# Attention and two expert layers on one core: V of the first batch pooled by products with a matrix of ones, more filler products, two normalisations moved to ScalarE, and a new list of slots

## The chip, the cores and the metric

The kernel runs on one core of one Trainium2 chip, as one program with one launch. The metric is device time in microseconds (us), from the first instruction to the last and what lies around them; the number before is a median of three runs. The engines are TensorE (PE, with its weight loads PEld), VectorE (DVE), ScalarE (ACT), GpSimd (POOL) and SyncE (SP), whose queue issues the DMAs.

## The reference

8 batches, 8 heads, 576 tokens, head size 64. K and V are averaged over groups of 8 tokens, which leaves 72 keys and 72 values for each head. The attended tokens (4608 of 512 numbers) go through two expert layers of 512 to 2048 to 512.

```python
k_p = k.reshape(B, H, Sp, pool, D).mean(axis=3)          # pool = 8, Sp = 72
v_p = v.reshape(B, H, Sp, pool, D).mean(axis=3)
scores = scale * np.matmul(q, k_p.transpose(0, 1, 3, 2))
scores = scores - np.max(scores, axis=-1, keepdims=True)
attn = np.exp(scores)
attn = attn / (np.sum(attn, axis=-1, keepdims=True) + 1e-09)
x = np.matmul(attn, v_p)                                 # then (4608, 512)
h = x @ w_in;   x = np.maximum(0.01 * h, h) @ w_out                  # layer 1
h = x @ w2_in;  x = (h * np.clip(h + 3.0, 0.0, 6.0) / 6.0) @ w2_out  # layer 2
```

## The kernel before

**Units of attention.** There are 24 units, three for each batch: unit 3b and unit 3b+1 take four heads each and the first 384 tokens (each with keys and values of its own to load), unit 3b+2 the other 192 tokens of all eight heads. A unit runs `scores` (products with the keys; a maximum, exponentials and sums in two halves of 432 columns; the normalisation at L633), `transposes` (L659), `transpose_rem` (L681; the last 8 keys of each head are handled apart) and `values` (L710). K is pooled by a reduction on DVE (L404). V is pooled so too, but for the first two units, `early`, TensorE does it in `pool_v` (L431): eight products with the identity, added up in PSUM, one for each token of a group of eight, first for 64 of the pooled values (128 columns each, `u.vs`) and then for the last 8 (32 partitions, 64 columns, `u.rs`). The copies of `u.vs` and the product of `u.rs` with a mask (L481) follow.

**Halves of the exponentials.** A half (number 2 times its unit, plus 0 or 1) is done in one of two ways: six exponentials on ACT, each with its maximum as bias and its sum read out (L599); or, where its number is in `C["sub"]`, a subtraction on DVE (L584), one exponential on ACT (L588) and a reduction on DVE (L591).

**The layers.** Layer 1 of the first 896 tokens is done by `moe_tile` in three passes: tokens 0 to 383 with the first 8 of 16 slices of the weights, tokens 384 to 895 with all 16, tokens 0 to 383 with the other 8. Meanwhile the weights are decoded and turned into the operands of a seven-product scheme, which are stored in DRAM (`first_weights`, `pair_weights`, `second_weights`, tensors `left...`). The other tokens of layer 1 and all of layer 2 go in nine `Pair`s of token blocks with those operands (L1158), streamed back from DRAM. The units of attention are spread over the three passes and the first pairs.

**The order.** The kernel is written as tasks with an engine, a cost and dependencies. A job is attached to a slot (one step of a pass or of a pair) by the tables in `C`, which sets the order in which tasks are written down and so which buffer each gets. `Plan.order` then simulates the engines with the costs, ranks the tasks by how long they may be delayed, and writes one fixed order for each engine; `flex` says up to which task a copy may go to either ACT or DVE. Up to `fill_until` (the third step of the first pass) it puts filler products of 128 zero columns (`self.fill`, L1654) in TensorE's queue: as many as fit a planned gap, and twelve more after a run of `weak` tasks (transposes, the scores of units 3b+2, the last 8 values). A filler is an instruction like others: if the gap is shorter than planned, what is behind it waits.

```python
out += [self.fill] * int((self.starts[i] - busy - 200) / 56)
busy = self.starts[i] + cost
if i in self.weak and weak > 1500:
    out += [self.fill] * 12
    weak = 0.0
weak = weak + cost if i in self.weak else 0.0
```

Of the kernel before, what the change touches and what calls it, by code (L numbers as in the profile page):

```python
# [16 lines left out]
ALU = mybir.AluOpType  # L17
AX = mybir.AxisListType

B, H, S, D = 8, 8, 576, 64  # L20
DM, DFF = 512, 2048
POOL, SP = 8, 72
# [9 lines left out]
C = dict(  # L32
    n32=4,
    soon={0: 0, 1: 0, 2: 2000},
    flex=715,
    mid=8,
    halves=9,
    sub=[1, 2, 3, 13, 20, 23],
    parts=31,
    when0=[0, 1, 0, 2, 5, 3, 10],  # L40
    att0=[0, 4, 8],
    gaps0=[0, 0, 2, 2, 0],
    when1=[4, 10, 20, 26],
    att1=[0, 7, 14, 22],
    gaps1=[0, 3, 3, 3, 0],
    att2=[0, 5],
    gaps2=[0, 1, 5, 6, 0],
    prep2=[26, 68],
    att=[[4, 26, 42, 51], [10, 24, 39, 58, 70], [0, 21, 40, 55], []],
    gaps=[[0, 7, 7, 11, 2], [0, 11, 9, 19, 1], [0, 2, 10, 11, 6], [7, 14, 2, 4, 4]],  # L50
    prep=[[85, 106], [94, 89], [102, 89], [84, 93]],
    left1=[[(0, 65)], [(1, 0), (2, 1), (3, 16)]],
    left2=[[], [], [(0, 40)], [(1, 23), (2, 45)], [(3, 18), (4, 39)], [(5, 23), (6, 40)], [(7, 15)]],
)
SCORES = 1500
WIDE_SCORES = 1400
# [50 lines left out]
class Plan:  # L107
# [102 lines left out]
    def order(self):  # L210
        n = len(self.tasks)
        ways, after = zip(*self.tasks)
        then = [[] for _ in range(n)]
        for i in range(n):
            for j in after[i]:
                then[j].append(i)

        due, pe = [0.0] * n, 0.0
        for i in range(n - 1, -1, -1):
            engine, cost, _ = ways[i][0]  # L220
            due[i] = min((due[j] - self.lag(engine, ways[j][0][0]) - self.extra[i] for j in then[i]), default=0.0)
            if engine == "pe":
                due[i] = pe = min(due[i], pe) - cost
            else:
                due[i] -= cost
        sooner = lambda rank: [r - self.sooner.get(i, 0) for i, r in enumerate(rank)]
        rank = sooner(i if w[0][0] == "pe" else d for i, (w, d) in enumerate(zip(ways, due)))
        back = lambda a, b: self.lag(b, a)
        self.end = None
        for _ in range(ROUNDS):  # L230
            starts, way, end = self.place(ways, after, then, rank, self.lag, FIRST)
            chosen = [w[k] for w, k in zip(ways, way)]
            if self.end is None or end < self.end:
                self.end, self.starts, self.chosen = end, starts, chosen
            late = [-s - w[1] for s, w in zip(starts, chosen)]
            starts, _, _ = self.place([[w] for w in chosen], then, after, late, back, {}, True)
            rank = sooner(-s - w[1] for s, w in zip(starts, chosen))
        self.idle = []
        out, busy, weak = [], WARM_FROM, 0.0
        for i in sorted(range(n), key=lambda i: (self.starts[i], i)):  # L240
            engine, cost, emit = self.chosen[i]
            if engine == "pe" and busy is not None:
                out += [self.fill] * int((self.starts[i] - busy - 200) / 56)
                busy = self.starts[i] + cost
                if i in self.weak and weak > 1500:
                    out += [self.fill] * 12
                    weak = 0.0
                weak = weak + cost if i in self.weak else 0.0
                if i == self.fill_until:
                    busy = None  # L250
            out.append(emit)
            self.idle.append((self.starts[i], i))
        return out


@with_exitstack
def attention_moe_moe(ctx: ExitStack, tc: tile.TileContext, qt, kt, vm, vr, wt, wq, eye, mask, out):

# [39 lines left out]
    def on_pe(n, emit, reads, writes, weak=False):  # L300
        if weak:
            plan.weak.add(len(plan.tasks))
        add("pe", n, emit, reads, writes)
# [25 lines left out]
    def load(dst, src, nbytes):  # L329

        on_dma(nbytes * (FIRST_LOADS if len(plan.tasks) < 60 else 1), lambda: DMA.dma_start(out=dst.ap(), in_=src), [], [dst])
# [39 lines left out]
        u.k, u.ks = a("k", lambda t: t[:, 0:1152]), a("ks", lambda t: t[:, 1152:1296])  # L371

    def raw_v(u, a):
        u.v, u.r = a("v", lambda t: t[:, 0:1024]), a("r", lambda t: t[:32, 1024:1536])
        u.vs, u.rs = a("vs", lambda t: t[:, 1536:1664]), a("rs", lambda t: t[:32, 1664:1728])
        u.m = u.m or a("m", lambda t: t[:32, 1728:1984])

# [9 lines left out]
    def fetch(u):  # L387
        if u.early:
            for i in range(2):
                load(half_k(u, i), kt[u.b, u.g, :, 576 * i : 576 * i + 576], 294912)  # L390
                load(half_q(u, i), qt[u.b, u.n, :, HALF * i : HALF * i + HALF], 196608)
        elif u.fresh:
            load(u.k, kt[u.b, u.g], 589824)
        if not u.early:
            load(u.q, qt[u.b, u.n], 393216)
        if u.fresh:
            load(u.v, vm[u.b, u.g], 524288)
            load(u.r, vr[u.b, u.g], 65536)

    def sum_pool(dst, src, n):  # L400

# [9 lines left out]
    def pair(t):  # L411
        return t.rearrange("p (a n) -> p a n", a=2)
# [10 lines left out]
    def pool_v(u):  # L423

        ps = buf("h", [128, 512], F32, 2, psum)
        u.vs, u.rs = ps("v", lambda t: t[:, 0:128]), ps("r", lambda t: t[:32, 128:192])
        for src, dst, n in ((u.v, u.vs, 128), (u.r, u.rs, 64)):

            def emit(src=src, dst=dst, n=n):
                for i in range(POOL):  # L430
                    PE.matmul(  # L431
                        out=dst.ap(),
                        lhsT=ident.ap()[: dst.ap().shape[0], : dst.ap().shape[0]],
                        rhs=src.ap()[:, i * n : i * n + n],
                        start=i == 0,
                        stop=i == POOL - 1,
                    )

            on_pe(1740 if n == 128 else 1320, emit, [src, ident], [dst], n < 128)

    held_keys, held_values, whole_v, whole_r = {}, {}, {}, {}

# [16 lines left out]
    def prep_v(u):  # L459
        if u.b == (1 if u.whole32 else C["n32"]):  # L460
            vbd[u.g] = [zeroed(f"vbd{u.g}0", F32)] if u.whole32 else [zeroed(f"vbd{u.g}{i}", F32R) for i in range(2)]
        held_values[u.g] = u.b
        if u.early:
            pool_v(u)
        else:
            sum_pool(u.vs, u.v, 128)
            sum_pool(u.rs, u.r, 64)
        for e in range(2):
            p = slice(64 * e, 64 * e + 64)
            s = View(u.vs.buf, u.vs.key, lambda t, p=p: pair(u.vs.cut(t))[p])  # L470
            if u.whole32:
                if u.b:
                    whole_v[u.g] = vbd[u.g][0]()
                copy(part(whole_v[u.g], e, lambda t, p=p: t[p, :, p]), s, 128, u.early, extra=0 if u.early else 100)
                continue
            hi, lo = [t(e, lambda t, p=p: t[p, :, p]) for t in vbd[u.g]]
            copy(hi, s, 128, extra=115)
            subtract(lo, s, hi, 128)
        on_dve(
            256,  # L480
            lambda: DVE.tensor_tensor(  # L481
                out=u.m.ap().rearrange("p (a d) -> p a d", a=4),
                in0=u.rs.ap().rearrange("p (o d) -> p o d", o=1).to_broadcast([32, 4, D]),
                in1=wide(mask_sb.ap(), D),
                op=ALU.mult,
            ),
            [u.rs, mask_sb],
            [u.m],
        )
        if u.b == 0:  # L490
            whole_r[u.g] = u.m
            return
        r = vrm[u.g]
        rows = [r(i, lambda t, i=i: t[32 * i : 32 * i + 32]) for i in range(3)]
        copy(rows[0], u.m, 256)
        copy(rows[1], u.m, 256)
        subtract(rows[2], u.m, rows[0], 256)

    def scores(u):
# [127 lines left out]
        else:  # L627
            u.rem = src

        flat = lambda: s.get()[:, 0 : NC * 256]  # L630
        on_dve(
            768,
            lambda: DVE.tensor_tensor(  # L633
                out=flat().rearrange("p (a k) -> p a k", k=64), in0=s3()[:, :, 0:64], in1=wide(inv.ap(), 64), op=ALU.mult
            ),
            [*whole, inv],
            whole,
        )
        u.p = lambda c, pi: flat()[:, 256 * c + 128 * pi : 256 * c + 128 * pi + 128]
        u.whole = whole  # L640

# [861 lines left out]
    place(u0)  # L1503
    raw_k(u1, a15)
    raw_v(u1, a14)
    u1.banks = [("y2", 1), ("y3", 1)]
    u0.other = {"r": [("y1", 1)]}
    u1.other = {"t": u1.banks, "v": u1.banks, "r": [("y1", 1)]}
# [10 lines left out]
    for k in keys:  # L1519
        add("gp", 400, lambda k=k: GP.memset(k.ap(), 0.0), [], [k])  # L1520
    fetch(u0)
    load(ident, eye, 65536)
    load(mask_sb, mask, 512)
    fetch(u1)
# [183 lines left out]
```

## Time and profile before

| | |
|---|---|
| median of three runs | 1561.88 us (1561.93, 1561.88, 1557.24) |
| profiled execution, its own time | 1557.78 us |
| its span, first to last instruction | 1556.0 us |
| PE busy | 1547.5 us (99%) |
| PEld busy | 1377.0 us (88%) |
| DVE busy | 1195.9 us (77%) |
| ACT busy | 998.8 us (64%) |
| DMA queue 1 | 433.18 MB, 80.0% of 16 engines |

Instruction groups are named by line, engine and tiles (out<-in). A product on 32-bit numbers (the attention's) shows as two records of MATMUL, one on the rounded numbers of the layers as one. The records of TensorE overlap: a record's own duration is longer than the distance to the next, so the pace is read from start to start, and waits of less than a record's tail hide in busy time. What lies around the span is 1.78 us (1557.78 less 1556.0).

### The profile page before, as it was taken

How to read it: one execution, taken by the hardware profiler on the slowest of the kernel's cores; microseconds unless marked ns; L12 is line 12 of the kernel's file. 1: busy time of each engine (PE TensorE's matmuls, PEld its weight loads, DVE VectorE, ACT ScalarE, POOL GpSimd, SP SyncE). 2: the span in 40 equal slices, each digit the busy share in tenths (PEclk: the TensorE clock that was granted, in tenths of full speed). 3: DMA queues.
4: the chain of work that ended last, by engine and by line, in shares of the span. 5: the costliest groups of instructions: out<-in, count | busy, mean ns of one | idle time of the engine just before them, and what ended most of it. 6: DMA issues, size and time to landing. Idle time of an engine off the chain costs nothing.

```text
span 1556.0 us, 23050 instructions
## 1 busy us (share of the span) xinstructions
PE 1547.5 (99%) x7893; PEld 1377.0 (88%) x7893; DVE 1195.9 (77%) x2124; ACT 998.8 (64%) x2267; POOL 2.9 (0%) x14
## 2 busy tenths in 40 slices
PE   9999999999999999999999999999999999999999
PEld 7987898898889888888888999988888888888887
DVE  8999997599669877897597779559657945875494
ACT  7978777767777687776665656455545644564454
POOL 0000000000000000000000000000000000000000
PEclk9999999999999999999999999999999999999999
DMA  8999779998999889999997977756866675676664
GB/s 306 344 353 305 277 282 342 324 310 297 330 326 325 270 309 328 318 322 325 332 329 263 340 258 263 250 204 234 280 217 214 248 258 207 216 261 215 216 229 145
DMA packets 141140, 434.65 MB, mean 279 GB/s; under 512 B 14432, under 2 KB 56032, under 8 KB 122848
## 3 DMA queue, kind: packets, MB, share of 16 engines
q1 hardware_dynamic: 141024, 433.18, 80.0%
q8 instruction: 63, 1.03, 0.3%
q14 instruction: 53, 0.43, 0.1%
HBM read 345.57 MB, written 87.56 MB: 278 GB/s over the span
## 4 chain that ended last, share of the span: by engine, by line
PE 93%; DVE 3%; DMA 2%; ACT 2%; issue 0%; SPq 0%; ACTq 0%; DVEq 0%
PE y L1158 44%; PE h L1158 25%; PE a L1158 13%; PE a L710 2%; PE h L893 1%; PE a L515 1%; PE y L939 1%; PE y L937 1%; PE y L938 1%; PE h L895 1%; PE h L894 1%; DMA left<-w 1%; PE a L659 1%; PE a L532 1%; PE idle L1654 0%; DMA raw<-kt 0%
## 5 line engine op out<-in xcount | busy, mean ns | idle before, releaser
L1023 DVE TENSOR_TENSOR w<-y,w 128x464 f32<-128x464 f32 (+1 forms) x124 | 79.0, 637 | 117.0 <-PE y L1158 114.3
L317 ACT ACTIVATE gh<-w 128x464 fp32r<-128x464 f32 (+1 forms) x140 | 82.2, 589 | 66.7 <-PE y L1158 23.6
L1158 PE MATMUL y<-w,xh 128*128 128x464 f32 (+1 forms) x552 | 122.9, 372 | 0.0
L1023 DVE TENSOR_TENSOR w<-w 128x464 f32<-128x464 f32 (+1 forms) x184 | 112.5, 631 | 3.2 <-ACT w L911 2.8
L1158 PEld LDWEIGHTS y<-w,xh 128*128 128x128 f32 x552 | 103.1, 188 | 11.6
L1356 DVE SCALAR_TENSOR_TENSOR gl<-w,gh 128x464 fp32r<-128x464 f32 (+1 forms) x140 | 88.5, 633 | 24.3 <-ACT gh L317 23.9
L314 ACT CAST gh<-w 128x464 fp32r<-128x464 f32 x128 | 74.3, 582 | 45.8 <-PE y L1158 23.9
L324 DVE TENSOR_TENSOR gl<-w,gh 128x464 fp32r<-128x464 f32 x128 | 81.0, 635 | 15.4 <-ACT gh L314 15.1
L1158 PE MATMUL y<-w,xl 128*128 128x464 f32 (+1 forms) x408 | 92.0, 373 | 0.0
L1327 ACT ACTIVATE gh<-w,three 128x464 f32<-128x464 f32 (+1 forms) x60 | 40.9, 682 | 70.0 <-DVE w L1023 70.0
L1158 PEld LDWEIGHTS y<-w,xl 128*128 128x128 f32 x408 | 76.0, 188 | 8.8
L1023 DVE TENSOR_TENSOR w<-h,w 128x464 f32<-128x464 f32 (+1 forms) x52 | 33.2, 639 | 64.2 <-PE h L1158 61.5
L911 ACT ACTIVATE w<-w 128x464 f32<-128x464 f32 x96 | 57.1, 600 | 38.7 <-DVE w L1023 38.2
L314 ACT COPY w<-y 128x464 f32<-128x464 f32 (+2 forms) x105 | 57.1, 547 | 32.0 <-PE y L1158 31.4
L324 DVE TENSOR_TENSOR st<-raw,st 128x512 fp32r<-128x512 f32 x88 | 60.0, 684 | 17.6 <-ACT st L314 17.6
L1158 PE MATMUL y<-gh,raw 128*128 128x464 f32 (+1 forms) x224 | 69.8, 372 | 0.0
L324 DVE TENSOR_TENSOR w<-x,w 128x464 fp32r<-128x464 f32 (+1 forms) x96 | 59.6, 632 | 11.8 <-ACT w L314 11.8
L1158 PE MATMUL h<-w,xl 128*128 128x464 f32 (+1 forms) x300 | 67.9, 373 | 0.0
L599 ACT ACTIVATE s<-a,mx 128x72 f32<-128x72 f32 x204 | 62.3, 338 | 7.0 <-DVE mx L575 6.5
L1158 PE MATMUL y<-w,w 128*128 128x464 f32 x288 | 65.0, 375 | 0.3 <-DMA w<-left 0.3
L1158 PE MATMUL h<-w,xh 128*128 128x464 f32 (+1 forms) x288 | 64.5, 372 | 0.0
L317 ACT ACTIVATE sb<-w 128x464 fp32r<-128x464 f32 (+1 forms) x70 | 41.3, 591 | 35.5 <-DVE s L1356 16.2
(296 smaller groups left out, 4257.1 us busy)
## 6 DMA issues: line engine op xcount, KB each, us to landing
raw<-left SPq DMA_DIRECT2D x60, 1024.0 KB, 4.9
xl<-left SPq DMA_DIRECT2D x90, 512.0 KB, 5.3
left<-st SPq DMA_DIRECT2D x176, 256.0 KB, 5.4
xh<-left SPq DMA_DIRECT2D x86, 512.0 KB, 5.6
w<-left SPq DMA_DIRECT2D x74, 512.0 KB, 5.4
xh<-left SPq DMA_DIRECT2D x33, 1024.0 KB, 4.8
xl<-left SPq DMA_DIRECT2D x25, 1024.0 KB, 4.9
raw<-wq SPq DMA_DIRECT2D x16, 1024.0 KB, 7.4
```

What stands on the lines that cost most here:

```text
L314: a = lambda: ACT.copy(out=dst.ap(), in_=src.ap())
L317: a = lambda: ACT.mul(out=dst.ap(), in_=src.ap(), mul=scale)
L324: lambda: DVE.tensor_tensor(out=dst.ap(), in0=a.ap(), in1=f32(b.ap()), op=ALU.subtract),
L515: PE.matmul(out=to.get()[:, 2 * SP * i : 2 * SP * i + 2 * SP], lhsT=u.q.ap()[:, pi * HALF + CQ * c : pi * HALF + CQ * c + CQ], rhs=keys[u. ...
L532: PE.matmul(out=ps.get()[to, (2 * c + pi) * SP : (2 * c + pi) * SP + SP], lhsT=u.q.ap()[rows, pi * HALF + at_ : pi * HALF + at_ + to.stop ...
L599: ACT.activation(out=at()[:, c, h, :], in_=ps.get()[:, o : o + SP], func=AF.Exp, bias=mx.get()[:, c, h : h + 1], accum_out=sm.get()[:, 4 * ...
L710: PE.matmul(out=ps.get()[:, c0 : c0 + n], lhsT=l(), rhs=r.ap()[:, c0 : c0 + n], start=i == 0, stop=i == len(ops) - 1)
L911: lambda: ACT.activation(out=dst.ap(), in_=src.ap(), func=AF.Prelu, alpha=0.01),
L1023: on_dve(n, lambda: DVE.tensor_tensor(out=dst.ap(), in0=a.ap(), in1=b.ap(), op=op), [a, b], [dst])
L1158: PE.matmul(out=o, lhsT=l, rhs=r, start=first and i == m == 0, stop=last and i == len(left) - 1 and m == 2, skip_group_check=True,)
L1327: lambda: ACT.activation(out=r.ap(), in_=h.ap(), func=AF.Relu, bias=three.ap()),
L1356: lambda: DVE.scalar_tensor_tensor(out=lo.ap(), in0=v.ap(), scalar=1.0 / 6.0, in1=f32(hi.ap()), op0=ALU.mult, op1=ALU.subtract),
```

## The change

Five things are done.

1. V of the first two units comes in another layout: 64 pooled values times two halves of the group of eight on 128 partitions, and four blocks of 256 columns. `pool_v` multiplies each block with a 128 by 128 matrix that adds the two halves and gives the result twice (`ones_sb`), four products of 256 columns in all; the last 8 values come on 64 partitions and take one product of 256 columns (`ones_r`). Two loads for the matrices (64 KB and 8 KB) are added after the loads of unit 0. Costs in the plan go from 1740 and 1320 ns to 1880 and 480 ns.
2. Fillers: ten more wherever a planned gap is over 300 ns, and the dozen after weak tasks comes from 700 ns on instead of 1500.
3. In units 10 and 11 the normalisation goes from one DVE instruction of 768 columns to twelve on ACT of 64 columns, planned at 150 ns each.
4. Halves 10, 17 and 22 are added to `sub`.
5. The slots, gaps and preparation times of nearly all jobs are new, `flex` goes from 715 to 691, and `halves` and `parts` get larger values.

```diff
-    flex=715,
+    flex=691,
     mid=8,
-    halves=9,
-    sub=[1, 2, 3, 13, 20, 23],
-    parts=31,
-    when0=[0, 1, 0, 2, 5, 3, 10],
+    halves=30,
+    sub=[1, 2, 3, 10, 13, 17, 20, 22, 23],
+    parts=50,
+    norm=[10, 11],
+    when0=[0, 2, 0, 2, 8, 2, 11],
...
-    left1=[[(0, 65)], [(1, 0), (2, 1), (3, 16)]],
+    left1=[[(0, 66)], [(1, 5), (2, 6), (3, 26)]],
...
-                out += [self.fill] * int((self.starts[i] - busy - 200) / 56)
+                gap = self.starts[i] - busy
+                out += [self.fill] * (int((gap - 200) / 56) + (10 if gap > 300 else 0))
                 busy = self.starts[i] + cost
-                if i in self.weak and weak > 1500:
+                if i in self.weak and weak > 700:
...
-        u.vs, u.rs = ps("v", lambda t: t[:, 0:128]), ps("r", lambda t: t[:32, 128:192])
-        for src, dst, n in ((u.v, u.vs, 128), (u.r, u.rs, 64)):
-
-            def emit(src=src, dst=dst, n=n):
-                for i in range(POOL):
-                    PE.matmul(
-                        out=dst.ap(),
-                        lhsT=ident.ap()[: dst.ap().shape[0], : dst.ap().shape[0]],
-                        rhs=src.ap()[:, i * n : i * n + n],
...
-            on_pe(1740 if n == 128 else 1320, emit, [src, ident], [dst], n < 128)
+        u.vs, u.rs = ps("v", lambda t: t[:, 0:256]), ps("r", lambda t: t[:32, 256:512])
+
+        def emit():
+            for i in range(4):
+                PE.matmul(
+                    out=u.vs.ap(), lhsT=ones_sb.ap(), rhs=u.v.ap()[:, 256 * i : 256 * i + 256], start=i == 0, stop=i == 3
+                )
+
+        on_pe(1880, emit, [u.v, ones_sb], [u.vs])
+        on_pe(
+            480,
+            lambda: PE.matmul(out=u.rs.ap(), lhsT=ones_r.ap(), rhs=u.r.ap(), start=True, stop=True),
...
+        def scaled():
+            for i in range(12):
+                ACT.mul(out=flat()[:, 64 * i : 64 * i + 64], in_=s3()[:, i, 0:64], mul=inv.ap()[:, i : i + 1])
+
+        if number // 2 in C["norm"]:
+            add("act", 12 * 150, scaled, [*whole, inv], whole)
+        else:
...
+    load(ones_sb, ones[:, 0:128], 65536)
+    load(ones_r, ones[0:64, 128:160], 8192)
     load(ident, eye, 65536)
```

## Rows read from the trace of the kernel before

**Rows 1.** The page: busy time of each engine; granted clock in 40 slices.
```profile
PE 1547.5 (99%) x7893; PEld 1377.0 (88%) x7893; DVE 1195.9 (77%) x2124; ACT 998.8 (64%) x2267; POOL 2.9 (0%) x14
...
PEclk9999999999999999999999999999999999999999
```
**Rows 2.** Waits of PE: us in total, times, longest; three of eight.
```profile
PE a L710 <- DVE w L315: 1.5, 1, 1.5
...
PE a L681 <- ACT th L314: 0.6, 1, 0.6
...
PE y L1158 <- DMA w<-left: 0.3, 1, 0.3
...
```
**Rows 3.** Stretches of 26 us: busy PE, PEld, DVE, ACT, POOL (instructions), PEclk, DMA.
```profile
0.00:26.00 26.00, 23.01 (x236) 19.52 (x237) 19.54 (x42) 14.72 (x41) 2.31 (x12) 1.00 0.89 306
...
104.00:130.00 26.00, 25.38 (x120) 20.60 (x119) 23.71 (x46) 18.93 (x61) 0.00 (x0) 1.00 1.03 362
...
208.00:234.00 26.00, 26.00 (x178) 25.37 (x177) 25.88 (x50) 18.93 (x49) 0.62 (x2) 1.00 0.88 306
...
1014.00:1040.00 26.00, 26.00 (x125) 23.19 (x124) 14.35 (x24) 12.56 (x21) 0.00 (x0) 1.00 0.61 219
```
**Rows 4.** The chain that ended last, 0 to 262 us: start, length, what.
```profile
17.43 3.40 PE a L710 x8
...
25.95 1.01 PE h L431 x16
26.96 0.37 PE h L893
...
231.72 5.95 DMA w<-left
```
**Rows 5.** Timeline, 10 to 44 us: start, length, engine, line, tiles, shape [idle before].
```profile
10.26 1.08 PE L431 MATMUL h<-raw,ident 32*32 32x64 f32 x16
...
11.78 1.00 PE L515 MATMUL y<-keys,w 128*128 128x144 f32 x6 [0.28 <-ACT keys L317]
...
12.95 1.95 PE L431 MATMUL h<-raw,ident 128*128 128x128 f32 x16
...
38.38 0.59 PE L710 MATMUL a<-w,w 128*128 128x192 f32 x2
38.90 0.59 PE L710 MATMUL a<-tr,w 32*128 32x192 f32 x2
```
**Rows 6.** Fillers: the whole group, then the timeline around the first two places.
```profile
L1654 PE MATMUL idle<-zeros x117: 219/219/314, 1.0 to 33.2; 128*128 128x128 bf16 x117
...
0.98 4.90 PE L1654 MATMUL idle<-zeros 128*128 128x128 bf16 x57 [0.98 <-DVE three L1525]
...
5.48 0.26 ACT L317 ACTIVATE keys<-raw 64x72 f32<-64x72 f32 x1 [0.78 <-DVE raw L404]
...
5.85 0.97 PE L515 MATMUL a<-keys,q 128*128 128x144 f32 x6
...
6.66 1.11 PE L1654 MATMUL idle<-zeros 128*128 128x128 bf16 x17
6.86 0.61 DVE L575 TENSOR_REDUCE mx<-a 128x6 f32<-128x432 f32 x1 [1.19 <-PE a L515]
...
7.61 0.95 PE L515 MATMUL a<-keys,q 128*128 128x144 f32 x6
```
**Rows 7.** All of L633 and L599: duration ns min/median/max, first and last start.
```profile
L633 DVE TENSOR_TENSOR s<-s,inv x19: 940/951/959, 12.3 to 632.7; 128x768 f32<-128x768 f32 x19
...
L599 ACT ACTIVATE s<-a,mx x204: 304/333/398, 9.3 to 631.4; 128x72 f32<-128x72 f32 x102
```
**Rows 8.** Timeline around unit 10's normalisation and its transposes.
```profile
194.59 0.94 DVE L633 TENSOR_TENSOR s<-s,inv 128x768 f32<-128x768 f32 x1
...
196.76 0.82 PE L659 MATMUL a<-ident,s 128*128 128x128 f32 x6
```
**Rows 9.** DMA issues: tiles, count, KB each, median us to landing.
```profile
w<-vr SPq DMA_DIRECT2D x1, 64.0 KB, 10.4
```

More of the change, by code (lines that the diff above doesn't have):

```diff
@@ L34 @@
     soon={0: 0, 1: 0, 2: 2000},
-    flex=715,
+    flex=691,
     mid=8,
-    halves=9,
-    sub=[1, 2, 3, 13, 20, 23],
-    parts=31,
-    when0=[0, 1, 0, 2, 5, 3, 10],
-    att0=[0, 4, 8],
[L42 to L51, printed above, removed]
-    left1=[[(0, 65)], [(1, 0), (2, 1), (3, 16)]],
-    left2=[[], [], [(0, 40)], [(1, 23), (2, 45)], [(3, 18), (4, 39)], [(5, 23), (6, 40)], [(7, 15)]],
+    halves=30,
[3 more added lines that the diff above has]
+    when0=[0, 2, 0, 2, 8, 2, 11],
+    att0=[0, 4, 8],
+    gaps0=[0, 0, 0, 2, 3],
+    when1=[4, 18, 20, 26],
+    att1=[0, 5, 13, 21],
+    gaps1=[0, 0, 3, 3, 1],
+    att2=[0, 6],
+    gaps2=[0, 2, 4, 6, 1],
+    prep2=[27, 56],
+    att=[[0, 25, 42, 51], [10, 24, 39, 58, 69], [0, 22, 46, 54], []],
+    gaps=[[0, 7, 8, 11, 0], [0, 11, 9, 19, 0], [0, 1, 8, 9, 14], [3, 14, 0, 0, 0]],
+    prep=[[95, 114], [99, 90], [103, 84], [93, 100]],
+    left1=[[(0, 66)], [(1, 5), (2, 6), (3, 26)]],
+    left2=[[], [], [(0, 36)], [(1, 23), (2, 43)], [(3, 16), (4, 52)], [(5, 27), (6, 38)], [(7, 4)]],
 )
@@ L256, in attention_moe_moe @@
 @with_exitstack
-def attention_moe_moe(ctx: ExitStack, tc: tile.TileContext, qt, kt, vm, vr, wt, wq, eye, mask, out):
+def attention_moe_moe(ctx: ExitStack, tc: tile.TileContext, qt, kt, vm, vr, vr0, wt, wq, eye, ones, mask, out):
     nc = tc.nc
@@ L373, in raw_v @@
     def raw_v(u, a):
-        u.v, u.r = a("v", lambda t: t[:, 0:1024]), a("r", lambda t: t[:32, 1024:1536])
+        u.v = a("v", lambda t: t[:, 0:1024])
+        u.r = a("r", lambda t: t[:64, 1024:1280] if u.early else t[:32, 1024:1536])
         u.vs, u.rs = a("vs", lambda t: t[:, 1536:1664]), a("rs", lambda t: t[:32, 1664:1728])
@@ L397, in fetch @@
             load(u.v, vm[u.b, u.g], 524288)
-            load(u.r, vr[u.b, u.g], 65536)
+            load(u.r, vr0[u.g] if u.early else vr[u.b, u.g], 65536)
     def sum_pool(dst, src, n):
@@ L425, in pool_v @@
         ps = buf("h", [128, 512], F32, 2, psum)
-        u.vs, u.rs = ps("v", lambda t: t[:, 0:128]), ps("r", lambda t: t[:32, 128:192])
-        for src, dst, n in ((u.v, u.vs, 128), (u.r, u.rs, 64)):
-            def emit(src=src, dst=dst, n=n):
-                for i in range(POOL):
-                    PE.matmul(
-                        out=dst.ap(),
-                        lhsT=ident.ap()[: dst.ap().shape[0], : dst.ap().shape[0]],
-                        rhs=src.ap()[:, i * n : i * n + n],
-                        start=i == 0,
-                        stop=i == POOL - 1,
-                    )
-            on_pe(1740 if n == 128 else 1320, emit, [src, ident], [dst], n < 128)
+        u.vs, u.rs = ps("v", lambda t: t[:, 0:256]), ps("r", lambda t: t[:32, 256:512])
[8 more added lines that the diff above has]
+            lambda: PE.matmul(out=u.rs.ap(), lhsT=ones_r.ap(), rhs=u.r.ap(), start=True, stop=True),
+            [u.r, ones_r],
+            [u.rs],
+            True,
+        )
     held_keys, held_values, whole_v, whole_r = {}, {}, {}, {}
@@ L469, in prep_v @@
             p = slice(64 * e, 64 * e + 64)
-            s = View(u.vs.buf, u.vs.key, lambda t, p=p: pair(u.vs.cut(t))[p])
+            if u.early:
+                s = View(u.vs.buf, u.vs.key, lambda t, p=p, e=e: u.vs.cut(t)[p].rearrange("p (a e d) -> p a e d", a=2, e=2)[:, :, e, :])
+            else:
+                s = View(u.vs.buf, u.vs.key, lambda t, p=p: pair(u.vs.cut(t))[p])
             if u.whole32:
@@ L482, in prep_v @@
                 out=u.m.ap().rearrange("p (a d) -> p a d", a=4),
-                in0=u.rs.ap().rearrange("p (o d) -> p o d", o=1).to_broadcast([32, 4, D]),
+                in0=u.rs.ap().rearrange("p (a d) -> p a d", a=4)
+                if u.early
+                else u.rs.ap().rearrange("p (o d) -> p o d", o=1).to_broadcast([32, 4, D]),
                 in1=wide(mask_sb.ap(), D),
@@ L630, in scores @@
         flat = lambda: s.get()[:, 0 : NC * 256]
[L631 to L638, printed above, removed]
+        def scaled():
[3 more added lines that the diff above has]
+            add("act", 12 * 150, scaled, [*whole, inv], whole)
+        else:
+            on_dve(
+                768,
+                lambda: DVE.tensor_tensor(
+                    out=flat().rearrange("p (a k) -> p a k", k=64), in0=s3()[:, :, 0:64], in1=wide(inv.ap(), 64), op=ALU.mult
+                ),
+                [*whole, inv],
+                whole,
+            )
         u.p = lambda c, pi: flat()[:, 256 * c + 128 * pi : 256 * c + 128 * pi + 128]
@@ L1505, in attention_moe_moe @@
     raw_v(u1, a14)
+    ones_sb, ones_r = a15("ones", lambda t: t[:, 1296:1424]), a15("ones_r", lambda t: t[:64, 1424:1456])
     u1.banks = [("y2", 1), ("y3", 1)]
@@ L1677 @@
     kt = k.reshape(B, 2, 2, 2, S, D).transpose(0, 1, 3, 5, 2, 4)
-    vv = v.reshape(B, 2, 2, 2, SP, POOL, D).swapaxes(5, 6)
-    vm = vv[:, :, :, :, :64].transpose(0, 1, 3, 4, 2, 5, 6)
-    vr = vv[:, :, :, :, 64:].reshape(B, 2, 32, POOL * D)
-    vm, vr = c(vm).reshape(B, 2, 128, 128, POOL), vr.reshape(B, 2, 32, D, POOL)
-    vm[0], vr[0] = [a[0].swapaxes(2, 3).reshape(a[0].shape) for a in (vm, vr)]
+    vv = v.reshape(B, 2, 2, 2, SP, POOL, D)
+    vm = vv[:, :, :, :, :64].transpose(0, 1, 3, 4, 2, 6, 5)
+    vr = vv[:, :, :, :, 64:].swapaxes(5, 6)
+    vm, vr = c(vm).reshape(B, 2, 128, 128, POOL), c(vr).reshape(B, 2, 32, D * POOL)
+    early = vv[0].reshape(2, 2, 2, SP, 4, 2, D)[:, :, :, :64]
+    vm[0] = early.transpose(0, 5, 3, 4, 1, 2, 6).reshape(vm[0].shape)
+    vr0 = vv[0, :, :, :, 64:].transpose(0, 4, 3, 1, 2, 5).reshape(2, 64, 256)
+    ones = np.zeros((128, 160), np.float32)
+    ones[:, 0:128] = np.tile(np.eye(64), (2, 2))
+    ones[:64, 128:160] = np.tile(np.eye(8), (8, 4))
     wi = moe_w_in.reshape(4, 128, NF, 128).transpose(2, 1, 0, 3).reshape(NF, 128, 512)
@@ L1693 @@
         "vm": c(vm.reshape(B, 2, 128, 2 * POOL * D)),
-        "vr": c(vr),
+        "vr": vr,
+        "vr0": c(vr0),
         "wt": c(np.concatenate([wi, wo], axis=2)).view(np.int64),
@@ L1697 @@
         "eye": np.eye(128, dtype=np.float32),
+        "ones": ones,
         "mask": c(mask),
```

## The prediction

> **What bounds the kernel now.** I read the page first. TensorE is busy for 1547.5 of 1556.0 us, DVE for 77% of the span, and the granted clock reads full, 2.4 GHz, in every slice [rows 1]. As records overlap, busy time alone proves little, so the view of waits came next: its eight lines of PE add up to 4.7 us, the longest being 1.5 us at the first V products, the longest after the start 0.6 us, and the wait for the first streamed operands 0.3 us [rows 2]. Then stretches of 26 us. In the pairs 125 products go in each stretch, 0.208 us each, with weight loads at 23 of 26 us: nothing is left there [rows 3]. In the passes DVE comes close to TensorE: from 208 to 234 us both are full (25.88 and 26.00), from 104 to 130 us TensorE lacks 0.62 us [rows 3]. The start is the loose part: in the first 26 us PE is busy 23.01 us, and much of that is filler [rows 3, 6]. The chain that ended last runs through TensorE, DVE and ACT in turn there, and later through the load of the first pair's operands at 231.7 us [rows 4].
>
> So the work of TensorE after 34 us is the same before and after, and only two things can move the time: the length of the start, and the few us of waits in the passes.
>
> **The last 8 values.** Each of the two early units loses 16 records that take 1.08 us and gets one product of 256 columns, two records. The nearest row is the identity product of 128 columns: 16 records in 1.95 us, which is 0.95 ns for a column and record, so 2 x 256 columns take 0.49 us. The farthest is the 192-column product of `values`: 0.52 us from start to start for two records [rows 5], and its 384-column sister takes 0.85 (3.40 us for four products) [rows 4]; between them 256 columns would take 0.63. The saving is 0.45 to 0.59 us a unit. In unit 0 it is covered: behind the old group TensorE stands idle at 11.78 anyway, until ACT has the keys [rows 5]. In unit 1 the group lies on the chain, at 25.95, with the first pass behind it [rows 4]. Term: -0.5, between -1.2 (both units) and 0.
>
> **The 64 pooled values.** Eight products of 128 columns become four of 256, 1024 columns either way. At the rate of the old ones, which also add up with weights of ones from the same tiles, it is 1.95 us before and after [rows 5]; at the 0.63 us of the far row four take 2.5 us, 0.55 more in each unit. I take the nearer row. Term: 0, between -0.1 and +1.1. Copies and the mask product keep their sizes.
>
> **The loads.** 72 KB more stand in the first queue. At 306 GB/s [rows 3] they hold what follows by 0.24 us, and two more issues stand ahead on SP. What hides them is the slack of unit 1's V: issued at the back of the queue, its last 64 KB take 10.4 us to land [rows 9], yet are used only at 25.95 [rows 4]. Term: 0; without that cover +0.3.
>
> **The fillers.** All 117 lie before 33.2 us [rows 6]. The 57 first go from 0.98 to 5.85 us, 85 ns each, the next 17 from 6.66 to 7.61, 56 ns each: TensorE starts below full speed, although the granted clock reads 1.00, and is at full speed from there on. Ten more are 0.56 us. Groups of 2, 9 and 6 follow, so five places have planned gaps over 300 ns: 2.8 us of filler in the queue. Behind the first group nothing is idle: the keys are there at 5.74 (5.48 plus 0.26), the scores start at 5.85, and DVE has waited 1.19 us for them at 6.86 [rows 6]. Ten more there come on top in full, +0.56. Elsewhere DVE is busy with other units, and the last group ends in the wait of 1.5 us [rows 2], which swallows it. With the lower threshold perhaps one more dozen falls in, 0.67. Term: +0.6, between 0 (the new plan has shorter gaps) and +2.9 (2.8 less 0.56, plus 0.67).
>
> **Two normalisations on ACT.** One DVE instruction of 0.95 us [rows 7] becomes twelve on ACT. The nearest row of 72 columns takes 0.26 us with a fixed scale [rows 6], 0.33 with a bias from memory [rows 7]: 3.1 to 4.0 us for the twelve, against the 1.8 of the plan. So unit 10 would be ready 2.2 us later or more. Before, 1.2 us lie between its end (195.53) and the transposes (196.76) [rows 8]; the new slots move these, and the other work of ACT has slack (18.93 of 26 us where DVE has 25.88) [rows 3]. Term: 0; if the cover fails, 1.0 us or more of wait in each of the two units, +2.0; relief of DVE is worth up to -0.6, the longest late wait.
>
> The Trainium skill speaks against this move: "ScalarE: Activation LUTs", Rules for kernel authors, puts multiplications on VectorE, and its section What ACT_TABLE_LOAD costs gives 280 ns + 0.833 ns a column with an operand from memory, less 93 of overlap, an estimate of 2.9 us for the twelve. By that price the sum stays as it is, since the rows already say that the twelve are slower and only their cover matters.
>
> **Three more halves with a subtraction.** Six exponentials of 0.33 us become one on ACT, and DVE gets two instructions of about 0.6 each (the reduction of 432 columns at 6.86 takes 0.61 [rows 6]), 1.2 us in each of units 5, 8 and 11. DVE is the fuller engine in the passes [rows 3]; the two normalisations give 1.9 us back of 3.6. Term: 0, between 0 and +1.2.
>
> **Slots, flex, halves, parts.** `halves` does nothing: it is compared with slices 0 to 7, and 9 covered these. `parts` does nothing either: it counts only up to `fill_until`, two slices away from the start. The slots and `flex` change the order, not the work. What they can win is the late waits, 1.7 of the 4.7 us, and 0.3 or so hidden in busy time, 2.0 in all; what they can lose by a late operand is of the same kind. Term: -1.0, between -2.0 and +2.0.
>
> **Sum.** -0.5 + 0 + 0 + 0.6 + 0 + 0 - 1.0 = -0.9: 1557.78 becomes 1556.9 in an execution like the profiled one. That one lies 4.1 us under the median; of the four executions two lie near 1557.5 and two near 1561.9, on average 1.9 above the profiled one. So a median of a few runs is 1558.8. A measurement of this kernel can tell about 0.3%, 4.7 us, from no change: under 1557.2 is faster, over 1566.6 slower.
>
> **The rivals.**
>
> *The fillers take the spread away.* The 4.1 us between executions of this one program are more than any one wait of PE. If they come from a clock that falls in some executions after the 1.5 us of idleness and the transposes of the start, more fillers hold it, and all executions take 1556.9, faster by 0.32%. For it: the fillers and the K = 128 products go just there. Against: here the pace never falls after 6.66 us, and the granted clock reads 1.00 throughout. The Trainium skill bears on it: in "TensorE: Matmul & The Clock Gate", Part 4, a transpose does not count as a busy TensorE in the way a product does. No run here shows it yet.
>
> *The new slots take nearly all waits away.* The 1.5 and 0.6 us, the rest of the late ones, and the second half-us of the last 8 values, with no filler in the way: -2.0 -1.2 -1.5 = -4.7, which gives 1553.1, 1555.0 as a median: faster.
>
> *A late first pair: slower.* The first streamed operands load at 231.72, 5.95 us long, on the chain, with 0.3 us of wait [rows 2, 4]: no slack. `first_weights` 1 and 2, which make them, move from slots 0 and 1 to 5 and 6 of the third pass; a slot there is 12 products of 384 columns, 2.1 us at 0.172 each (the 0.208 for 464 columns [rows 3], scaled), so 10 us later if the planner doesn't pull them ahead. What is more than 0.3 us late stands in full on the end: 10 us give 1566.9, 1568.8 as a median. It decides from 8 us on (1566.6 less 1558.8). Against: a slot sets buffers and ties, the planner pulls late work forward.
>
> *No effect at all* (the start stays bound by loads, terms of either sign cancel) is inside the likeliest case.
>
> **How the numbers follow.** About the same as before, 1558.8: 0.52, its own range 1557.2 to 1562.5. Spread gone, 1556.9: 0.22. Waits gone, 1553 to 1555: 0.14. Late first pair: 0.12, of which some fall short of 1566.6. So faster 0.36, same 0.53, slower 0.11. The bounds of the terms add to -3.9 and +9.5, not likely together; 1552.5 to 1564.5 leaves out the late pair and little below.
>
> **What would show it.** Right: `pool_v` as 8 + 2 records in about 2.5 us a unit, more fillers before 34 us, the first pass's second slice within 1 us of before, no PE wait over 1 us after it. Wrong: 256-column records at 0.3 us each; the chain of the start through fillers at more than one place; PE waiting for ACT before the transposes of units 10 and 11; a wait at the first product of the pairs of some us; a pace of the fillers of 85 ns or more after the start.

## The result and the profile after

The changed kernel takes 1568.62 us (median of five, 1567.97 to 1570.0) beside 1560.73 of before in the same comparison: ratio 1.0055, interval 1.004 to 1.0069. It is slower, and 1568.62 lies outside the forecast range of 1552.5 to 1564.5. Its profiled execution took 1568.62 us with a span of 1566.8, 10.8 us longer than before.

The page after, busy time and the chain by engine, in answer to [rows 1]:

```profile
PE 1554.9 (99%) x7978; PEld 1382.6 (88%) x7978; DVE 1197.4 (76%) x2131; ACT 1003.9 (64%) x2255; POOL 2.9 (0%) x14
...
PE 93%; ACT 2%; DMA 2%; DVE 2%; issue 0%; SPq 0%; ACTq 0%; DVEq 0%
```

PE has 85 records more although `pool_v` lost records: these are fillers. The waits of PE after, in answer to [rows 2] (total, times, longest):

```profile
PE a L676 <- ACT s L643: 2.8, 4, 1.2
PE a L698 <- ACT th L316: 2.7, 3, 1.2
PE idle L1674 <- DVE three L1545: 1.0, 1, 1.0
PE y L1175 <- ACT w L316: 0.8, 1, 0.8
```

The longest is new; the second, at the same transposes, was 0.6 us before (L681 there) [rows 2]. L643 is the twelve multiplications of a normalisation on ACT, L676 the transposes that read them, L698 the transposes of the last 8 keys, which wait until ACT, behind the twelve, has copied earlier transposes out of their bank (`th`). The 1.5 us wait at the first V products is gone, filled with fillers, and no wait for a DMA is left. Stretches of 26 us after, in answer to [rows 3]:

```profile
0.00:26.00 26.00, 24.90 (x270) 21.61 (x271) 17.83 (x40) 12.51 (x34) 2.31 (x12) 1.00 0.93 310
...
104.00:130.00 26.00, 26.00 (x124) 21.32 (x123) 25.92 (x50) 20.12 (x58) 0.00 (x0) 1.00 1.05 360
182.00:208.00 26.00, 23.45 (x126) 20.12 (x125) 22.41 (x40) 19.54 (x56) 0.00 (x0) 1.00 0.77 282
208.00:234.00 26.00, 25.09 (x164) 23.83 (x162) 23.67 (x45) 17.00 (x39) 0.00 (x0) 1.00 0.80 258
234.00:260.00 26.00, 23.15 (x120) 20.23 (x121) 18.24 (x35) 19.61 (x63) 0.62 (x2) 1.00 0.95 336
```

In the first 26 us PE is busier than before and DVE and ACT do less: the queue is longer, the work later. From 182 to 260 us PE lacks 6.3 us (26.00 three times less 23.45, 25.09 and 23.15); in the trace of before it lacks 0.33 there. The start, PE alone:

```profile
0.98 5.77 PE L1674 MATMUL idle<-zeros 128*128 128x128 bf16 x67 [0.98 <-DVE three L1545]
...
7.38 1.67 PE L1674 MATMUL idle<-zeros 128*128 128x128 bf16 x27
...
9.68 1.67 PE L1674 MATMUL idle<-zeros 128*128 128x128 bf16 x27
...
13.72 1.78 PE L1674 MATMUL idle<-zeros 128*128 128x128 bf16 x29
...
15.66 1.89 PE L433 MATMUL h<-raw,w 128*128 128x256 f32 x8
...
18.00 0.62 PE L440 MATMUL h<-raw,w 64*32 64x256 f32 x2
...
37.07 0.42 PE L910 MATMUL h<-xh,w 128*128 128x384 f32 x1
```

The new products came out as priced: 8 records in 1.89 us and 2 in 0.62 (with the tail of the last), where [rows 5] had 16 in 1.95 and 16 in 1.08. But 246 fillers stand here instead of 117, and the chain that ended last runs straight through them. A part of it, start, length, what:

```profile
7.54 1.51 PE idle L1674 x27
9.05 0.79 PE a L525 x6
9.84 1.51 PE idle L1674 x27
11.35 0.79 PE y L525 x6
12.14 0.95 PE idle L1674 x17
```

No wait for data stands between: the scores wait for fillers. In e1 below, the same order with the old fillers, the third group of scores does wait for data, 0.8 us for a load of its queries, so that much of the filler there hides a wait. And around unit 10, the timeline after, in answer to [rows 8]:

```profile
200.44 4.39 ACT L643 ACTIVATE s<-s,inv 128x64 f32<-128x64 f32 x12
...
202.60 0.33 PE L676 MATMUL a<-ident,s 128*128 128x128 f32 x1 [0.17 <-ACT s L643]
...
204.12 0.33 PE L676 MATMUL a<-ident,s 128*128 128x128 f32 x1 [1.19 <-ACT s L643]
...
207.01 0.54 PE L698 MATMUL a<-ident,rem 128*96 128x128 f32 x3 [1.18 <-ACT th L316]
```

Twelve multiplications take 4.39 us, 0.366 each on average, against 0.15 in the plan, and the transposes are queued into the middle of them.

Marks on TensorE in the profiled execution of each kernel, in us from the span's start, carry the rest. The pass of tokens 384 to 895 is the one with products of 512 columns.

| run | second slice of the first pass starts | 512 columns, first | 512 columns, last | first streamed product | span |
|---|---|---|---|---|---|
| before | 33.19 | 80.61 | 191.52 | 233.30 | 1556.0 |
| after | 37.07 | 84.33 | 194.44 | 243.80 | 1566.8 |
| e1 old fillers | 32.95 | 80.37 | 190.49 | 238.44 | 1563.0 |
| e2 normalisation on DVE | 38.05 | 85.26 | 195.36 | 240.21 | 1562.9 |
| e3 both undone | 33.38 | 80.73 | 190.87 | 234.55 | 1559.1 |
| e4 ones alone, planned anew | 32.09 | 80.27 | 193.51 | 239.59 | 1562.7 |
| e6 before, new fillers | 34.97 | 82.38 | 191.61 | 233.35 | 1555.7 |
| e7 before, ACT normalisation | 33.27 | 80.67 | 190.81 | 241.72 | 1565.1 |
| e10 before, 20 fillers at one place | 34.26 | 81.60 | 191.68 | 233.42 | 1557.2 |
| e11 before once more | 33.16 | 80.53 | 189.26 | 231.03 | 1553.8 |

The 10.8 us of the change arise in two steps: +3.88 by 37 us, and from +2.92 at the end of the second pass to +10.5 at the first streamed product. The pairs keep that to 0.4 us.

Marks of single executions have a scatter of their own. e11 is the same program as before, and its second pass takes 108.73 us instead of 110.91 (191.52 less 80.61). In e10 everything in the start is 1.1 us later from the first product on, because the pace of the first fillers rose at 6.8 us instead of 4.3. So a difference of 1 to 2 us at one mark proves nothing by itself. The second step stands: from the last product of 512 columns to the first streamed one it is 49.36 us after, and 41.78 and 41.77 in the two executions of before.

### The profile page after: what moved, and what is told of

Read it like the earlier page. It is cut to its first block, busy times and chain, and to the rows that moved or that the text cites. A ratio compares the mean times of both kernels' runs of the same rounds, so it can differ in the third digit from the quotient of the medians.

```text
span 1566.8 us, 23242 instructions
## 1 busy us (share of the span) xinstructions
PE 1554.9 (99%) x7978; PEld 1382.6 (88%) x7978; DVE 1197.4 (76%) x2131; ACT 1003.9 (64%) x2255; POOL 2.9 (0%) x14
## 4 chain that ended last, share of the span: by engine, by line
PE 93%; ACT 2%; DMA 2%; DVE 2%; issue 0%; SPq 0%; ACTq 0%; DVEq 0%
PE y L1175 43%; PE h L1175 24%; PE a L1175 13%; PE a L727 2%; PE a L525 1%; PE h L910 1%; PE h L912 1%; PE h L911 1%; PE idle L1674 1%; DMA left<-st 1%; PE y L954 1%; PE y L956 1%; PE y L955 1%; PE a L676 1%; PE a L542 1%; DMA raw<-wq 1%
## 5 line engine op out<-in xcount | busy, mean ns | idle before, releaser
L609 ACT ACTIVATE s<-a,mx 128x72 f32<-128x72 f32 x192 | 58.5, 340 | 9.5 <-DVE mx L585 9.4
```

What stands on the lines that cost most here:

```text
L609: ACT.activation(out=at()[:, c, h, :], in_=ps.get()[:, o : o + SP], func=AF.Exp, bias=mx.get()[:, c, h : h + 1], accum_out=sm.get()[:, 4 * ...
```

## The experiments

**e1, e2, e3: the fillers, the normalisations, both.** Fillers are put in after the plan is made, so e1 has the order of the changed kernel on every engine; e2 keeps the task at its place and cost and issues the one DVE instruction there.

```diff
# e1
-                out += [self.fill] * (int((gap - 200) / 56) + (10 if gap > 300 else 0))
+                out += [self.fill] * int((gap - 200) / 56)
-                if i in self.weak and weak > 700:
+                if i in self.weak and weak > 1500:
# e2
-            for i in range(12):
-                ACT.mul(out=flat()[:, 64 * i : 64 * i + 64], in_=s3()[:, i, 0:64], mul=inv.ap()[:, i : i + 1])
+            DVE.tensor_tensor(...)      # the 768 columns at once
# e3: both
```

> The changed kernel with the filler rule of before (no ten extra, the dozen from 1500 ns on); fillers are put in after the plan is made, so the order of all else is the same. Theory (extra fillers delay the start, the normalisations on ACT delay the third pass): the second slice of the first pass starts at about 33.2 us instead of 37.07, the time falls by 3.9 us to about 1564.7. Rival (the fillers hold the clock): the pace of products after 6 us falls, the start is no shorter, time 1568 or more. Rival (the start waits for loads, fillers only fill): no change, 1568.6.

> The changed kernel with its order kept, but at the place of the twelve ACT multiplications of units 10 and 11 stands one DVE multiplication of 768 columns, with the new fillers. Theory: the four waits of PE around the transposes of these units (5.5 us) go, and the first streamed product starts 6 to 7 us earlier than 243.8: time about 1562. Rival (the new slots themselves are worse there, whichever engine does it): the waits move to DVE and less than 2 us is won, 1567.

> The changed kernel with the old filler rule and the normalisations at the same places on DVE: products with ones, slots, three more halves remain. Theory (the two losses add): 3.9 + 6.5 less than 1568.6, 1558, which is no change against before within its spread. Rival (slots worse): 1562 or more. Rival (products with ones and slots win by themselves): under 1555.

Beside these three and e4 ran 26 executions of before, their companions, with a median of 1558.44: e1 1563.54, ratio 1.0029 (1.0017 to 1.0041); e2 1565.27, 1.0044 (1.0026 to 1.0061); e3 1559.11, 1.0003 (0.9993 to 1.0013). The fillers are worth 5.1 us of the median (1568.62 less 1563.54, from two comparisons) and 4.1 at the mark (37.07 less 32.95). The normalisations are worth 4.4 us (1563.54 less 1559.11); from the last product of 512 columns to the first streamed one it is 47.95 us in e1 and 43.68 in e3, 4.3 less. e2 won less than was expected of it; its start was 1 us later than that of the changed kernel (the pace of its first fillers rose later, see the last section), and against e3 it shows the fillers again. With both undone the median can't be told from that of before, and the first theory holds.

At the same granted clock something is left. All twelve executions of e3 ran at 1.0. Of the 26 companions, 14 ran at 0.999 or more, with a median of 1557.4; the other 12, at 0.997 and 0.998, took 1559.5 to 1562.2. Beside the 14, e3 is 1.7 us slower: products, slots and halves together cost that much, and the fallen clock of the 12 hides most of it. So the parts are 5.1 for the fillers, 4.4 for the normalisations and 1.7 for the rest, 11.2 in all, near the 10.8 of the two profiled executions, which both had the full clock; the medians show 7.9 (1568.62 less 1560.73).

In e2 the waits for L643 are gone, one of a usual kind takes a part of their place:

```profile
PE a L699 <- DVE rem L326: 1.0, 1, 1.0
PE a L699 <- ACT th L316: 0.8, 2, 0.5
```

**e4, e5: the products with ones.** e4 is the kernel before with the new products, planned anew under the old slots. e5 keeps the old costs and dependencies in the plan, so that the order on every engine is that of before, with two more loads on SP.

```diff
# e5, against e4
-        on_pe(1880, emit, [u.v, ones_sb], [u.vs])
+        on_pe(1740, emit, [u.v, ident], [u.vs])
-            480,
+            1320,
-            [u.r, ones_r],
+            [u.r, ident],
# and the two loads are issued inside ident's task
```

> The kernel before with the products with ones alone (its slots, its filler rule, normalisations on DVE). Theory: one product instead of sixteen records on the chain of unit 1 wins 0.5 us, less what the new plan fills with fillers: 1557 to 1561, not to be told from before; records of 256 columns at 0.22 us. Rival (256 columns cost 0.3 us a record and the loads of the matrices delay the start): second slice later than 33.2 us by 1 us or more.

> The kernel before in exactly its own order on every engine, with only the V products of the first two units replaced by the products with ones (and the two loads ahead of ident on SP). Theory (the products themselves win 0.5 us or nothing, and what the run with ones alone lost was its new plan): second slice at 32.5 to 33.2 us, waits as before, 1557 to 1559 beside 1558.4 of before. Rival (the products or the two loads cost 5 us): 1562 or more.

e4: 1563.87, ratio 1.0031 (1.0019 to 1.0043), a loss that neither side had foreseen whole. Its start is 1.1 us shorter (32.09 against 33.19), records of 256 columns go at 0.216 us. What it loses comes later: it is 2.0 us behind at the end of the second pass (no more than two executions of before differ), and loses 4.3 more from there to the first streamed product. It has waits that the kernel before does not have, the first of them once in the second and once in the third pass:

```profile
PE y L955 <- DVE gl L326: 1.9, 2, 1.0
PE a L525 <- ACT xa L319: 1.4, 1, 1.4
```

e5: 1561.93, ratio 1.0014 (1.0001 to 1.0027), but from 1557.7 to 1566.73 over twelve executions. The share of the clock that each was granted sorts them: at 0.999 and more 1557.7 to 1558.2, at 0.996 to 0.998 1560.2 to 1566.7. The profiled one (1565.16) shows the place. Timeline, PE:

```profile
34.93 0.34 PE L912 MATMUL h<-xh,w 128*128 128x384 f32 x1
37.20 0.50 PE L698 MATMUL a<-ident,rn 128*32 128x128 f32 x3 [1.93 <-ACT w L316]
...
38.27 0.53 PE L910 MATMUL h<-xh,w 128*128 128x384 f32 x1
38.59 0.53 PE L911 MATMUL h<-xl,w 128*128 128x384 f32 x1
```

and stretches of 4 us of the same run:

```profile
32.00:36.00 4.00, 3.27 (x26) 2.90 (x23) 3.33 (x6) 1.58 (x4) 0.00 (x0) 1.00 1.04 415
36.00:40.00 4.00, 2.80 (x11) 2.35 (x11) 2.41 (x5) 3.97 (x10) 0.00 (x0) 0.72 1.03 400
40.00:44.00 4.00, 4.00 (x10) 2.25 (x10) 2.64 (x5) 2.11 (x6) 0.00 (x0) 0.50 1.04 417
```

After a wait of 1.93 us the granted clock falls to 0.50, 1.2 GHz, and products of 384 columns go 0.32 us apart instead of 0.175 until 51.5 us; the second pass starts at 88.4 instead of 80.6. So the median of e5 does not give the price of the products. Its three executions at 0.999 and more lie among the 17 companions at that clock (1555.3 to 1559.5, median 1557.5): as far as three can tell, the products win nothing that can be measured, and their own cost is not 5 us. Why the clock falls in nine of twelve here, and in 12 of 29 companions, is not shown.

**e6, e7: fillers and ACT normalisation in the order of before.** Each is the kernel before with one edit, the filler rule or the twelve multiplications, everything else in its old place.

> The kernel before in its own order with only the new filler rule (ten more where a planned gap is over 300 ns, the dozen from 700 ns on). Theory: 50 to 60 more fillers, some 3 us, of which 1.5 to 3 end on the chain of the start: second slice at 34.7 to 36.2 us, 1560 to 1561.5. Rival (DVE and ACT set the start, fillers hide): no later than 33.5, no change.

> The kernel before in its own order with only the normalisations of units 10 and 11 as twelve ACT multiplications at the same places. Theory (4.4 us of ACT in place of 0.95 of DVE, whatever the slots): PE waits 2 us or more before the transposes of each unit, and the first streamed product starts 4 to 6 us later than 233.3: 1562.5 to 1564.5. Rival (only the new slots left it without cover; here 1.2 and 2.3 us of slack lie before the transposes): under 1560.5.

e6: 1559.18, ratio 1.0001 (0.999 to 1.0013). The start is 1.8 us longer as expected, and yet the time is not: 33.19 becomes 34.97, 80.61 becomes 82.38, but the second pass ends at 191.61 against 191.52. From 104 to 130 us, where PE lacked 0.62 us in [rows 3], it is now full, as if DVE had set the pace there before and the second pass had swallowed the delay. But in e11, the kernel before once more with its start unchanged, PE is full there as well, and the second pass ends at 189.26. First e6, then e11:

```profile
104.00:130.00 26.00, 26.00 (x124) 21.31 (x123) 25.50 (x49) 19.91 (x67) 0.00 (x0) 1.00 1.03 355
104.00:130.00 26.00, 26.00 (x123) 21.28 (x122) 25.73 (x52) 20.64 (x65) 0.00 (x0) 1.00 1.05 365
```

So the 0.62 us belong to one execution and not to the kernel, and beside e11 the span is longer by as much as the start (1555.7 against 1553.8). The granted clock explains the equal times: e6 ran at 0.999 or more in all twelve, with a median of 1559.2, and the 17 companions at that clock have 1557.5. At the same clock the longer start costs 1.6 us (by two medians of executions that lie 4 to 5 us apart); the other 12 companions, at 0.997 and 0.998, bring the time of before up by about as much.

e7: 1569.1, ratio 1.0059 (1.0042 to 1.0076), worse than was expected. Here the transposes wait, then a product of the pass for ACT's activation, which is queued behind the twelve:

```profile
193.87 4.39 ACT L634 ACTIVATE s<-s,inv 128x64 f32<-128x64 f32 x12
...
197.55 0.55 PE L661 MATMUL a<-ident,s 128*128 128x128 f32 x3 [1.12 <-ACT s L634]
...
200.24 0.69 PE L895 MATMUL h<-x,w 128*128 128x384 f32 x1 [1.60 <-ACT u L913]
```

Within the last of these waits the clock falls, to 0.50 from 199.3 to 206.1 us, which adds some 3.4 us (an estimate, half of 6.8); the first streamed product starts 8.4 us later than in the trace of before. All five executions had 0.996 to 0.998.

**e8, e10, e11: what fillers are for.** e8 is e3 with fillers ahead of the first product only. e10 is before with 20 more at one place, the wait of 1.5 us. e11 is before once more, for its profile.

```diff
# e8
+                out += [self.fill] * (int((gap - 200) / 56) if busy == WARM_FROM else 0)
-                if i in self.weak and weak > 1500:
+                if i in self.weak and weak > 10**9:
# e10
+                if i in self.hold:
+                    out += [self.fill] * 20
```

> The changed kernel's order with the normalisations on DVE and fillers only ahead of the first product, none after it. Theory (fillers after the start only delay): second slice at 31.5 to 33 us instead of 33.38, 1557 to 1559. Rival (fillers hold the clock): products of the start at half pace, 432 ns for a record of 256 columns, second slice at 35 us or later, 1561 or more.

> The kernel before in its own order with 20 more fillers (1.1 us) at one place only, ahead of the first V product, where TensorE waits 1.5 us for DVE. Theory (part of the spread of before is a clock that falls after idleness in the start, and this is the longest idleness): clock 1.0 in nearly all executions, no delay, median 1556.7 to 1557.5. Rival (the fall comes from a later wait, at 34 to 37 us): clock 0.998 in about half of the executions as before, 1558.5.

> The kernel before once more, for its profile alone. Theory: where its clock falls (an even chance in one execution) it does so at 34 to 52 us, after a wait of some 2 us for ACT or DVE, as in the run with its order and the products with ones, and the time is 1560 to 1562.5; where it does not fall, 1555.5 to 1558. Rival: it falls elsewhere, or 1560 and more comes with the clock at full.

e8: 1560.56, ratio 1.0012 (1.0001 to 1.0023), clock under 1.0 in five of twelve executions, against none of e3's twelve. The start is 1.1 us shorter (32.30 against 33.38), the median is no better. e10: 1559.55, ratio 1.0002 (0.9994 to 1.0011): its clock stays at 0.999 or more in eleven of twelve, but seven of these still took over 1559, so the median is no better. At its place the wait swallows the 20 fillers: it falls from 1.5 to 0.4 us, and the first V product starts 1.07 us later (18.50 against 17.43) where the first product of all was already 1.09 later (6.94 against 5.85). e11 had the full clock and 1555.54 us: the place at which the clock of before falls was not seen. That it falls is seen: of 29 executions beside e5 to e8, the 12 at 0.997 to 0.998 took 1559.6 to 1562.5 us and the 17 others 1555.3 to 1559.5. These 17 still lie 4.2 us apart, so the clock is a part of the spread and not all of it.

**e9: the true price.** e1 with the normalisation planned at 12 x 366 ns.

```diff
-            add("act", 12 * 150, scaled, [*whole, inv], whole)
+            add("act", 12 * 366, scaled, [*whole, inv], whole)
```

> The changed kernel with the old filler rule, the normalisations on ACT, but planned at 12 x 366 ns as measured instead of 12 x 150, so the whole order is planned again. Theory (the wrong price is what failed; with the true one the planner moves other work ahead): waits before the transposes of units 10 and 11 under 1 us, 1559 to 1561. Rival (4.4 us on ACT cannot be hidden there, or any new plan under slots made for another one loses): 1562.5 or more.

1566.77, ratio 1.005 (1.0033 to 1.0067). The theory that the planned price alone failed falls: planned anew, the transposes still wait, and the clock falls twice, at 203 and at 237 us, for 3.4 us each. As the whole order is new, the 3.2 us by which e9 lies over e1 are not the price's alone.

```profile
PE a L676 <- ACT s L643: 3.0, 5, 1.2
PE h L912 <- DVE w L326: 1.2, 1, 1.2
```

**e12: the three halves.** e3 in the same order, with halves 10, 17 and 22 as six exponentials on ACT again.

> The kernel of the run with both losses undone (products with ones, new slots, old filler rule, normalisations on DVE), in the same order, but halves 10, 17 and 22 done by six exponentials on ACT as before. Theory (the three halves are worth nothing): 1558 to 1560.5 beside 1559.1. Rival (they are a part of what the new slots need: ACT is too full for them): 1561 or more. Rival (they load DVE for nothing): under 1557.5.

1560.52, ratio 1.001 (1.0001 to 1.002), where e3 had 1.0003 (0.9993 to 1.0013). The intervals overlap; the halves are worth 1 us or nothing.

## Why the prediction was wrong

**The last 8 values, the 64 values, the loads: right.** 0.62 us with the tail instead of 1.08, 216 ns a record instead of the 0.3 of the far row, loads that nobody waits for. Under the old slots the start is 1.1 us shorter (e4, 137 fillers). In the changed kernel's order the old rule puts in 152 fillers instead of 117, and little of it is left (32.95 in e1, 33.38 in e3, 33.19 before).

**The fillers: the term was mis-sized, +0.6 for +4.1 at the mark (5.1 in the median).** I counted five planned gaps in the order of before; that order has six, and no new dozen (e6: 177 fillers, 60 more). The new plan has its own: seven places with ten more and two dozens, 246 less the 152 of e1, 94 fillers or 5.3 us. And I let all but the first ten vanish because DVE was busy elsewhere; the chain above goes through every one of them, since the scores that they hold up are what DVE and ACT work on next. Right was that the wait of 1.5 us swallows fillers put right ahead of it (e10). The bound of +2.9 did not hold the term either. All upper bounds together, +9.5, would have given 1569.2 as a median (1557.78 and 9.5 and 1.9); the range left that out as not likely.

**The two normalisations: the step "Term: 0" failed; they cost 4.3 to 4.4 us.** The multiplication was priced by 72 columns with a fixed scale or a bias, 0.26 to 0.33 us; with a scale from memory the twelve took 4.39, 0.366 each. That is the lesser error. I judged the cover by the slack between one instruction and the transposes, and by ACT's share of busy time. But the twelve stand as one block of 4.4 us in ACT's order, and the work of ACT behind it, the copies of the transposes and the pass's activations, is late as well, which PE waits for in turn (2.7 us at L698 after, 1.6 at L895 in e7). e9 shows that a true price does not mend it. The Trainium skill's rule to use VectorE for multiplications ("ScalarE: Activation LUTs", Rules for kernel authors) agrees with these runs (4.4 us, e1 against e3). The estimate of 2.9 us for the twelve, worked out from the figures in the section What ACT_TABLE_LOAD costs of that page of the Trainium skill, does not: the trace has 4.39.

**Slots: the term -1.0 compared the wrong things.** Against before they win nothing: e3, which has them, is at 1.0003, and at the same clock 1.7 us behind. But e4, the same products under the old slots and halves, is at 1.0031, 4.8 us over e3, and the halves account for 1 us of that or nothing (e12). A change of a cost makes another plan, and what the new slots win goes into getting back what that plan lost. That slots fit one plan only is argued from this one pair.

**"Only two things can move the time: the length of the start, and the few us of waits in the passes"** named the right places, 3.9 us in the start and 7.6 before the first streamed product. That the start passes on nearly in full holds too: in e6 1.8 us more of it cost 1.6 at the same clock. What failed is that the waits were taken as a small stock, 2.0 us to win or to lose; two blocks on ACT made more than that.

**The rivals.** That fillers hold the clock was right as a mechanism in the order of before: e6 ran at 0.999 or more in twelve of twelve executions, its companions of before in 17 of 29. The changed kernel ran at 0.999 to 1.0, but its order has a part in that: e3 holds the clock with 152 fillers, and e8 in ten of twelve with 57. Two things failed. The clock is not all of the spread: e6 still goes from 1557.1 to 1561.9. And the price was left out: the fillers cost in the start what they save. The late first pair gave nearly the measured time (1568.8) by luck, for a reason that is not there: PE's first streamed product is 10.5 us late, but no DMA is among its waits.

Not settled: what the new slots alone do in a plan without the rest, where the clock of before falls in those executions in which it does, which part of products, slots and halves costs the 1.7 us of e3, and what makes two executions of before at full clock 2.2 us different in the second pass.

## What to carry to other kernels

Price a filler as an instruction in the queue of the engine that feeds the others, count it in the new plan's gaps and not in the old one's, and then look whether a wait right behind it swallows the delay, as the one in e10 did. A block of small instructions moved to an engine with spare time costs what stands behind the block, not what the engine's busy share suggests: name the next instructions of that engine and who waits for them. When a planner writes the order, test each edit in the old order first: e4 and e5 have the same products, and the new plan of e4 is 5.8 us slower than the three executions of e5 at full clock. And compare executions at the same granted clock: the equal times of e6 and of before hid 1.6 us.

## What the runs showed of the hardware

- The pace of the first fillers goes from 107 to 56 ns a piece at 3.7 to 7.0 us from the start, differently in each execution (4.3 in before and 4.5 in e11, the same code), while the granted clock reads 1.00. A fixed number of fillers thus lasts longer when the pace rises late: 67 of them until 6.59 us in the changed kernel, until 7.57 in e2, where it rose at 7.0.
- A fall of the granted clock to 1.2 GHz 0.6 us after a wait of 1.9 us, in a start with waits of 0.8 and 1.5 us before it (e5), and within a wait of 1.6 us that follows waits of 1.1 and 0.2 (e7). It held for 13.7 and 6.8 us. The view of a run's mean clock, 0.996 and 0.998, is enough to tell such executions apart.
- ACT's multiplication of 64 columns by a value from memory: 348 ns each. Of the twelve of unit 10 after, the second starts 253 ns behind the first, the third 365 behind the second, and the others lie 380 to 382 ns apart; the whole takes 4.39 us.
